# Chunk 0 of a linear-attention and PReLU kernel: scores and outputs as whole 128x128 products, k by tokens through transposes, longer idle products

## The chip, the cores and the metric

The kernel runs on one core of one Trainium2 chip. The metric is the device time of one execution in microseconds (us). The core has a TensorE (PE; its weight loads are listed as PEld), a VectorE (DVE), a ScalarE (ACT), a GpSimd (POOL) and a queue on SyncE (SP) that issues the DMAs. Each engine runs its own list of instructions in order and waits for the others by semaphores. TensorE's clock is granted at one of two levels, 2.4 GHz (1.00 in the profile) or 1.2 GHz (0.50).

## What is computed

```python
for t in range(S):                       # S = 768 tokens, B = 4, H = 8, D = 48
    kt, vt, rt = k[:, :, t], v[:, :, t], r[:, :, t]
    cur = einsum('bhd,bhe->bhde', u * kt, vt)
    y[:, :, t] = einsum('bhd,bhde->bhe', rt, state + cur)
    state = w * state + einsum('bhd,bhe->bhde', kt, vt)
x = y as (B*S, 384)
h = x @ w_in                             # 384 -> 2048
g = maximum(h, 0) + alpha * minimum(h, 0)
out = g @ w_out                          # 2048 -> 384
```

## The kernel before

The 768 tokens are cut into six chunks of 128. In each chunk the recurrence is written as products: r and k are scaled by powers of w (tables `W[m]`), the scores k.r of the chunk are masked to the strictly earlier tokens, their diagonal is filled with a sum over r.k.u, and the outputs are scores by v. What a chunk leaves behind is a state `T`, made of k by tokens (`kk`) and v. The eight heads go as four pairs, q = 0 to 3; a pair's two heads lie on partitions 0 to 47 and 64 to 111.

Chunk 0 has no state before it. `first_chunk` writes a pair's work: r and k0 are scaled on DVE (L431), their product is summed on PE (`c_sum`, L526) and goes through ACT to `cu` (L530). `scores` on PE works in half chunks of 64 tokens: 16 products of 64x64 for the two diagonal blocks (L445) and 8 for the block between them (L449). The mask's other side, `base`, is the identity times cu: four ACT instructions for one head (L462) and one DVE instruction for the other (L456, `BY_DVE`). DVE copies the masked scores over it (L466), ACT copies the block between to `off` (L470, shown as gl). `out` on PE (L480) takes 16 products for the tokens of the first half and then, behind an ACT reading of the same bank (`seen_y`, L486), 8 for the second half. The result is split in two terms (`xh`, `xl`) by ACT and by a PE product with minus the identity (`splits_by_pe`, L393), and DMAs (`lower`) bring one pair's rows to their places. `state` then writes k by tokens with real products against a diagonal matrix `spread` that holds w^128 (`by_tokens`, L298) and the state's own product (L508).

The two dense layers follow. They come as steps: `m_in` is nine products of 512 columns (L689), `m_out` nine more (L722); 96 steps, 1728 products. Their weights are unpacked on ACT and DVE (`weights`, L346 to L357), sixteen blocks, the first two while chunk 0 runs. The attention of chunks 1 to 5 is put between the steps in bursts (`burst`).

What sets the order: every piece of work is put into a plan with its engine, its cost in us and a rank (`add`); `in_order` walks through the pieces with those costs and writes one list for each engine. `warm` is an idle product: 256 columns of the identity into a spare bank, whose result nobody reads. `with_warm(n, ...)` puts n of them ahead of a piece, 33 stand at the start, and after planning each gap that the plan shows ahead of the first dense product gets more. Chunk 0's pairs 0 and 2 keep `base` in a pool of three buffers, which the masked scores of later chunks use too.

Of the kernel before, what the change touches and what calls it, by code (L numbers as in the profile page):

```python
# [18 lines left out]
L = 128  # L19
# [12 lines left out]
BY_DVE = (1,)  # L32
# [146 lines left out]
def rwkv_prelu_kernel(ctx: ExitStack, tc, rk, vkr, wP, uP, u, wall, alpha, w, r_all, k_all, v_all, oT):  # L179
# [26 lines left out]
    one, unit, ones = fixed([128, 2], "one"), sb([112, 65], "g", 3), sb([128, 128], "g", 3)  # L206
# [15 lines left out]
    const.tile([128, 32], F32, name="space")  # L222
# [8 lines left out]
    def warm(into):  # L231
        x = ident().bitcast(mybir.dt.bfloat16)
        nc.tensor.matmul(into()[:, 256:512], x[:, 0:128], x, start=True, stop=True, skip_group_check=True)  # L233

    def with_warm(n, us, fn, r, w, rank):

        p = add("PE", us + 0.107 * n, lambda: [warm(bank) for _ in range(n)] + [fn()], r=r + [ident] * (n > 0),
            w=w + [(bank, ("warm", len(plan.pieces)))] * (n > 0), rank=rank)
        p.warm = n

# [3 lines left out]
    def load(out, fn, kb, rank, behind=()):  # L244
# [19 lines left out]
        w=[ones], rank=-100)  # L264
    for g in range(2):
# [18 lines left out]
    def spreads():  # L284

        add("ACT", 0.3, lambda: nc.scalar.activation(minus(), ident()[0:112, 0:112], AF.Copy, scale=-1.0), r=[ident],
            w=[minus], rank=-60)
        for m in range(P):
            add("ACT", 0.3, lambda m=m: nc.scalar.activation(
                spread()[:, m], ident()[0:112].rearrange("p (g e) -> p g e", g=2)[:, :, 0:D], AF.Copy,  # L290
                scale=W[m]()[:, L:L + 1]), r=[ident, W[m]], w=[(spread, m)], rank=-59 + m)

    def by_tokens(q, k0, k, rank, behind=()):
# [7 lines left out]
        add("PE", 0.77, product, r=[k0, (spread, q)], w=[t], rank=rank).after.update(behind)  # L301
# [4 lines left out]
    def half_table():  # L306
# [3 lines left out]
        for m in range(P):  # L310
            for j in range(2):
                add("ACT", 0.3, lambda m=m, j=j: nc.scalar.activation(
                    rows()[:, m, HI * j:HI * (j + 1)], W[m]()[:, L - 1:HI - 1:-1], AF.Copy, scale=W[m]()[:, L:L + 1]), r=[W[m]],
                    w=[(rows, (m, j))], rank=-21).after.update(last_out)
        for m in range(P):
            add("PE", 0.15, lambda m=m: nc.tensor.transpose(
                pt()[:, 128 * m:128 * m + 112], rows()[:, m], ident()[0:112, 0:112]),
                r=[(rows, (m, j)) for j in range(2)] + [ident], w=[(pt, m)], rank=-20)
# [101 lines left out]
    def first_chunk(q):  # L420
# [17 lines left out]
        lo, hi = slice(0, HI), slice(HI, L)  # L438

        def scores():  # L440
            for b in range(B):
                at = slice(b * HI, (b + 1) * HI)
                for g in range(2):
                    for s in (lo, hi):
                        nc.tensor.matmul(A[g]()[s, at], k0()[half(g), b, s], r()[half(g), b, s], start=(b == 0),  # L445
                                         stop=(b == B - 1), skip_group_check=True)
            for b in range(B):
                for g in range(2):
                    nc.tensor.matmul(A[g]()[lo, 256 + b * HI:256 + (b + 1) * HI], k0()[half(g), b, lo], r()[half(g), b, hi],  # L449
                                     start=False, stop=(b == B - 1), skip_group_check=True)  # L450

        with_warm(3, 0.95, scores, r=[r, k0], w=A, rank=q - 90)
        base, off = sb([128, 2, B, HI], "base", 3), sb([128, 2, B, HI], "gl", 3, F32, mv)
        for g in range(2):
            if g in BY_DVE:
                add("DVE", 0.42, lambda g=g: nc.vector.tensor_tensor(  # L456
                    out=base()[:, g], in0=ident2()[:, None, :].broadcast_to([128, B, HI]),
                    in1=cu()[:, g, :, None].broadcast_to([128, B, HI]), op=ALU.mult), r=[cu, ident2],
                    w=[(base, (g, b)) for b in range(B)], rank=10 * q - 77 + g)
                continue  # L460
            for b in range(B):
                add("ACT", 0.32, lambda g=g, b=b: nc.scalar.activation(  # L462
                    base()[:, g, b], ident2(), AF.Copy, scale=cu()[:, g, b:b + 1]), r=[cu, ident2],
                    w=[(base, (g, b))], rank=-60 + q)
        for g in range(2):
            add("DVE", 0.44, lambda g=g: nc.vector.copy_predicated(  # L466
                base()[:, g], strict2()[:, None, :].broadcast_to([128, B, HI]),
                A[g]()[:, 0:256].rearrange("p (b t) -> p b t", b=B)), r=[strict2, A[g]],
                w=[(base, (g, b)) for b in range(B)], rank=10 * q - 76 + g)
            add("ACT", 0.42, lambda g=g: nc.scalar.activation(  # L470
                off()[lo, g].rearrange("p b t -> p (b t)"), A[g]()[lo, 256:512], AF.Copy), r=[A[g]], w=[(off, g)],
                rank=-59.5 + q)
        y = psum()

        def out(rows, pieces):
            for b in range(B):
                for g in range(2):
                    to, x = (lo if g == 0 else half(g)), g * B + b
                    for n, (t, j) in enumerate(pieces):
                        nc.tensor.matmul(y()[to, b * L + HI * j:b * L + HI * (j + 1)], v().rearrange("p x e -> p (x e)")[  # L480
                            rows, x * D:x * D + to.stop - to.start], t()[rows, g, b], start=(rows == lo and b == n == 0),
                            stop=(b == B - 1), skip_group_check=True)

        with_warm(2, 0.78, lambda: out(lo, ((base, 0), (off, 1))), r=[v, base, off], w=[y], rank=q - 85)

        add("ACT", 0.2, lambda: nc.scalar.activation(  # L486
            seen_y()[:, 0:2], y()[HI:HI + 1, B * L - 2:B * L], AF.Copy), r=[y], rank=-99)
        last_out[:] = [add("PE", 0.42, lambda: out(hi, ((base, 1),)), r=[v, base], w=[y], rank=q - 85.1)]
# [10 lines left out]
        def state():  # L499
            by_tokens(q, k0, k, -40 + q, last_out)  # L500
            U = psum()

            def product():
# [7 lines left out]
            add("PE", 0.47, product, r=[k, v], w=[U], rank=0.5 * q + 0.2)  # L511
            T[q] = sb([112, B, D], "T", 9)
            add("ACT", 0.4, lambda t=T[q]: nc.scalar.activation(t(), u_rows(U, 0), AF.Copy, scale=W[q]()[:, L:L + 1]),
                r=[U, W[q]], w=[T[q]], rank=0.5 * q + 0.2)
        return state

    def diagonal(q, r, k0, cu, sums, cols, mine, prod_rank, sum_rank, copy_rank):
# [11 lines left out]
        with_warm(3 if mine != sums else 0, 0.45, c_sum, r=[prod, uw], w=[mine], rank=sum_rank)  # L529
# [50 lines left out]
    def burst(i, was, at):  # L580
# [66 lines left out]
        first = add("PE", (0.7 if before else 0.1) + (0.8 if now else 0.1), run, r=uses, w=writes, rank=at)  # L647
        if before:

            row, col = (HI, L) if joint else (0, L)  # L650
            seen = add("ACT", 0.2, lambda: nc.scalar.activation(
                seen_y()[:, 0:2], y[1]()[row:row + 1, col + HI - 1:col + HI + 1], AF.Copy), r=[y[1]], rank=at - 200)
            seen.soon[first] = 0.75
# [29 lines left out]
    def m_in(n):  # L683
        c, i = STEPS[n]
        hp = psum("hp", 2)
        for k in range(NK):
# [6 lines left out]
            add("PE", 0.7, mm, r=[wh[i], wl[i]] + [(t[c], (kx, p)) for t in (xh, xl) for kx in need for p in range(6)],  # L693
# [266 lines left out]
```

## Time and profile before

| | us |
|---|---|
| median of three runs | 505.71 (504.98 to 506.17) |
| the profiled execution's own time | 506.03 |
| its span, first to last instruction | 504.3 |
| PE busy in the span | 492.1 (98%) |
| DVE, ACT, POOL busy | 310.8, 243.1, 41.9 |
| first dense product (L689) on PE | 44.6 after the span's start |

The page gives busy times over the whole span; views by stretch give each engine's busy time, the granted clock and the share of the DMA engines. In the chain of work that ended last each row is a start, a length and what ran then, and a row "issue" is time in which an engine waited for nothing that the profile shows. A product of 32-bit floats has two records in the trace, and one of the rounded kind that the dense layers use has one.

### The profile page before, as it was taken

Reading aid. Unit: us, or ns where it says so; the run is one execution under the profiler, and the core shown is the slowest. Engines: PE = TensorE matmul, PEld = TensorE weight load, DVE = VectorE, ACT = ScalarE, POOL = GpSimd, SP = SyncE. Lnnn points to the kernel's source line nnn. Section 1 sums busy time; section 2 is a strip of 40 time slices with the busy share of each in tenths; the row PEclk is TensorE's granted clock in tenths of the full one; section 3 lists DMA queues with packets and bytes.
Section 4 is the critical chain, followed back from the end, with each engine's and each line's share of the span. In section 5 each row is a group of like instructions: output and inputs, shape, how many; then the busy total and the mean of one; then the engine's idle time right before and its main releaser. Section 6 shows DMA issues by size and latency. Waiting matters only on the chain.

```text
span 504.3 us, 11838 instructions
## 1 busy us (share of the span) xinstructions
PE 492.1 (98%) x4949; PEld 404.8 (80%) x4949; DVE 310.8 (62%) x522; ACT 243.1 (48%) x565; POOL 41.9 (8%) x48
## 2 busy tenths in 40 slices
PE   8899999899999999999999999999999999999994
PEld 6688888678888888888888888888888887888883
DVE  7553988999988668586476466667544534333331
ACT  4556578566765555355345355444443324422222
POOL 1000001000321101110122020121000000000000
PEclk9856999999999999999999999999999999999999
DMA  7436267646314363141221131312030000100001
GB/s 216 160 89 207 99 199 217 183 164 215 108 50 154 101 199 113 56 147 39 89 74 53 53 130 48 97 57 69 20 96 1 1 1 1 63 0 1 0 1 68
DMA packets 23739, 45.87 MB, mean 91 GB/s; under 512 B 3968, under 2 KB 11264, under 8 KB 23680
## 3 DMA queue, kind: packets, MB, share of 16 engines
q1 hardware_dynamic: 23680, 45.05, 28.6%
q8 instruction: 41, 0.67, 0.6%
q14 instruction: 18, 0.15, 0.1%
HBM read 36.38 MB, written 6.29 MB: 85 GB/s over the span
## 4 chain that ended last, share of the span: by engine, by line
PE 95%; DVE 2%; DMA 1%; issue 1%; SPq 0%; ACT 0%; ACTq 0%
PE bank L689 39%; PE acc L722 39%; PE bank L627 3%; PE bank L637 2%; PE bank L298 2%; PE bank L480 2%; PE bank L606 2%; PE bank L599 2%; PE acc L233 1%; DMA raw<-rk 1%; PE bank L508 1%; PE bank L393 1%; DVE raw L549 0%; PE acc L526 0%; PE bank L526 0%
## 5 line engine op out<-in xcount | busy, mean ns | idle before, releaser
L698 DVE SCALAR_TENSOR_TENSOR g<-bank,alph,g 128x512 f32<-128x512 f32 x96 | 71.9, 749 | 109.8 <-ACT g L697 109.5
L697 ACT ACTIVATE g<-bank 128x512 f32<-128x512 f32 x96 | 57.2, 596 | 141.7 <-PE bank L689 141.5
L689 PE MATMUL bank<-xh,wh 128*128 128x512 f32 x288 | 113.5, 394 | 0.0
L689 PE MATMUL bank<-xh,wl 128*128 128x512 f32 x288 | 112.3, 390 | 0.0
L689 PE MATMUL bank<-xl,wh 128*128 128x512 f32 x288 | 112.1, 389 | 0.0
L702 DVE TENSOR_TENSOR gl<-g,gh 128x512 fp32r<-128x512 f32 x96 | 70.6, 736 | 38.3 <-ACT gh L701 37.6
L701 ACT ACTIVATE gh<-g 128x512 fp32r<-128x512 f32 x96 | 60.5, 630 | 64.2 <-DVE g L698 64.1
L722 PE MATMUL acc<-gh,wh 128*128 128x512 f32 x288 | 83.6, 397 | 1.6 <-ACT gh L701 1.6
L722 PE MATMUL acc<-gl,wh 128*128 128x512 f32 x288 | 81.4, 390 | 0.2 <-DVE gl L702 0.2
L722 PE MATMUL acc<-gh,wl 128*128 128x512 f32 x288 | 81.6, 390 | 0.0
L722 PEld LDWEIGHTS acc<-gl,wh 128*128 128x128 f32 x288 | 53.9, 188 | 11.9 <-DVE gl L702 0.7
L722 PEld LDWEIGHTS acc<-gh,wh 128*128 128x128 f32 x288 | 52.5, 188 | 13.5 <-ACT gh L701 2.4
L689 PEld LDWEIGHTS bank<-xl,wh 128*128 128x128 f32 x288 | 54.2, 188 | 11.3
L689 PEld LDWEIGHTS bank<-xh,wh 128*128 128x128 f32 x288 | 54.2, 188 | 11.4
L722 PEld LDWEIGHTS acc<-gh,wl 128*128 128x128 f32 x288 | 54.0, 188 | 11.5
L689 PEld LDWEIGHTS bank<-xh,wl 128*128 128x128 f32 x288 | 54.2, 188 | 11.1
L560 POOL TENSOR_TENSOR rr<-rr,kk 128x384 f32<-128x384 f32 x16 | 19.8, 1236 | 306.6 <-DMA kk<-vkr 164.7
L571 ACT ACTIVATE base<-ident,cu 128x64 f32<-128x64 f32 x160 | 41.3, 337 | 1.9 <-DVE cu L566 1.8
L382 DVE TENSOR_TENSOR xl<-bank,xh 48x256 fp32r<-48x256 f32 (+1 forms) x66 | 28.4, 430 | 3.8 <-ACT xh L381 2.5
L381 ACT ACTIVATE xh<-bank 48x256 fp32r<-48x256 f32 (+1 forms) x66 | 25.4, 385 | 2.9 <-PE bank L637 1.0
L549 DVE TENSOR_TENSOR raw<-raw,W 112x512 f32<-112x512 f32 x40 | 26.3, 680 | 0.8 <-DMA raw<-rk 0.8
L562 POOL TENSOR_TENSOR rr<-rr,utab 128x384 f32<-128x384 f32 x16 | 19.8, 1239 | 1.3
(107 smaller groups left out, 421.9 us busy)
## 6 DMA issues: line engine op xcount, KB each, us to landing
wraw<-wall SPq DMA_DIRECT2D x16, 768.0 KB, 4.6
raw<-rk SPq DMA_DIRECT2D x46, 224.0 KB, 3.6
v<-vkr SPq DMA_DIRECT2D x24, 192.0 KB, 3.8
kk<-vkr SPq DMA_DIRECT2D x16, 192.0 KB, 3.3
rr<-vkr SPq DMA_DIRECT2D x16, 192.0 KB, 2.5
oT<-o SPq DMA_DIRECT2D x12, 256.0 KB, 2.2
oT<-g SPq DMA_DIRECT2D x6, 256.0 KB, 2.6
xh<-xh SPq DMA_DIRECT2D x36, 32.0 KB, 2.0
```

What stands on the lines that cost most here:

```text
L381: add("ACT", us, lambda: nc.scalar.activation(to(h), view(), AF.Copy), r=[src], w=refs(h), rank=rank)
L382: add("DVE", us + 0.1, lambda: nc.vector.tensor_tensor(out=to(l), in0=view(), in1=to(h), op=ALU.subtract), r=[src] + refs(h), w=refs(l), r ...
L549: add("DVE", 0.72, lambda t=t, tab=tab: nc.vector.tensor_tensor(out=t().rearrange("p b (j t) -> p (b j) t", j=2), in0=t().rearrange("p b ( ...
L560: add("POOL", 1.2, lambda: nc.gpsimd.tensor_tensor(out=rt(), in0=rt(), in1=k(), op=ALU.mult), r=[k] + ([wh[12]] if c == 2 else []), w=[rt] ...
L562: add("POOL", 1.2, lambda: nc.gpsimd.tensor_tensor(out=rt().rearrange("p (g b) e -> p g b e", g=2), in0=rt().rearrange("p (g b) e -> p g b ...
L571: add("ACT", 0.32, lambda g=g, b=b: nc.scalar.activation(base()[:, g, b], ident2(), AF.Copy, scale=cu()[:, g, b:b + 1]), r=[cu, ident2], w ...
L689: nc.tensor.matmul(hp()[:, :], a[i]()[:, k], x[c]()[:, k], start=(k == 0 and j == 0), stop=(k == NK - 1 and j == 2))
L697: add("ACT", 0.6, lambda: nc.scalar.activation(g(), hp()[:, :], AF.Copy), r=[hp], w=[g], rank=n - 100)
L698: add("DVE", 0.75, lambda: nc.vector.scalar_tensor_tensor(out=g(), in0=hp()[:, :], scalar=alph()[:, i:i + 1], in1=g(), op0=ALU.mult, op1=A ...
L701: add("ACT", 0.64, lambda: nc.scalar.activation(gh(), g(), AF.Copy), r=[g], w=[gh], rank=n - 100)
L702: add("DVE", 0.73, lambda: nc.vector.tensor_tensor(out=gl(), in0=g(), in1=gh(), op=ALU.subtract), r=[g, gh], w=[gl], rank=n - 99)
L722: nc.tensor.matmul(banks[k](), a[i]()[:, NK + k], x(), start=(begin and j == 0), stop=(end and j == 2))
```

## The change

1. `scores` makes eight products of 128x128 a pair (L448 of the changed kernel) in place of 24 of 64x64, and `out` eight of K=128 and 128 columns (L469) in place of 24. The `seen_y` reading, `off` and its two ACT copies go.
2. `base` is a whole 128x128 block for each batch: eight ACT instructions a pair (L455), none on DVE; a pair takes two tiles of it, from the pool `base` for pairs 0 and 2, from `gl` for pairs 1 and 3. The two masked copies (L459) are 512 wide in place of 256.
3. Chunk 0's k by tokens is made by four plain transposes a pair and two ACT copies; w^128 comes in when the state leaves its bank (`w128`). Chunk 1 keeps `by_tokens`.
4. An idle product has 384 columns; a pair of chunk 0 has 2 + 2 + 3 + 2 = 9 of them in place of 8 of 256. The start has 23 in place of 33. A gap in the plan gets one for each 0.17 us, where it is over 0.25 us.
5. Costs in the plan change (dense products, bursts, the wait between a burst's halves), and so the order.

```diff
     def warm(into):
         x = ident().bitcast(mybir.dt.bfloat16)
-        nc.tensor.matmul(into()[:, 256:512], x[:, 0:128], x, start=True, stop=True, skip_group_check=True)
+        nc.tensor.matmul(into()[:, 128:512].rearrange("p (a f) -> p a f", a=2), x[:, 0:128],
+                         x[:, None, 0:192].broadcast_to([128, 2, 192]), start=True, stop=True, skip_group_check=True)
...
-        with_warm(3, 0.95, scores, r=[r, k0], w=A, rank=q - 90)
...
+        with_warm(2, 1.05, scores, r=[r, k0], w=A, rank=q - 90)
+        base = [sb([128, B, L], "gl", 3, F32, mv) if q % 2 else sb([128, B, L], "base", 3) for _ in range(2)]
+        for g in range(2):
+            for b in range(B):
+                add("ACT", 0.39, lambda g=g, b=b: nc.scalar.activation(
+                    base[g]()[:, b], ident(), AF.Copy, scale=cu()[:, g, b:b + 1]), r=[cu, ident], w=[(base[g], b)],
+                    rank=-60 + q)
...
+                    nc.tensor.matmul(y()[rows, b * L:(b + 1) * L], v().rearrange("p x e -> p (x e)")[
+                        :, x * D:x * D + rows.stop - rows.start], base[g]()[:, b], start=b == 0,
+                        stop=b == B - 1, skip_group_check=True)
+
+        last_out[:] = [with_warm(3, 0.95, out, r=[v] + base, w=[y], rank=q - 85)]
...
-            by_tokens(q, k0, k, -40 + q, last_out)
+            t = psum()
+
+            def turn():
+                for b in range(B):
+                    nc.tensor.transpose(t()[:, 112 * b:112 * (b + 1)], k0()[:, b], ident()[0:112, 0:112])
+
+            with_warm(2, 0.5, turn, r=[k0, ident], w=[t], rank=-40 + q).after.update(last_out)
...
-        with_warm(3 if mine != sums else 0, 0.45, c_sum, r=[prod, uw], w=[mine], rank=sum_rank)
+        with_warm(2 if mine != sums else 0, 0.56, c_sum, r=[prod, uw], w=[mine], rank=sum_rank)
...
-    add("PE", 7.0, lambda: [warm(bank) for _ in range(33)], r=[ident], w=[(bank, "warm")], rank=-1000)
+    add("PE", 6.7, lambda: [warm(bank) for _ in range(23)], r=[ident], w=[(bank, "warm")], rank=-1000)
```

The order on PE, ahead of the first dense product. Before, four pairs of real products (L298; rr is `spread`) and the states' products of the pairs stand there:

```order
L298 MATMUL bank_121<-rr,raw 128x96 x4
L298 MATMUL bank_119<-rr,raw 128x96 x4
L298 MATMUL bank_117<-rr,raw 128x96 x4
L298 MATMUL bank_118<-rr,o 128x96 x4
L508 MATMUL bank_121<-v,kk 64x48
L508 MATMUL bank_121<-v,kk 48x48
```

Now (L234 are idle products, L489 the transposes, L685 the dense ones, L503 the states' products):

```order
L489 MATMUL bank_117<-ident,raw 128x112 x4
L234 LDWEIGHTS ident
L234 MATMUL acc_135<-ident 128x384
...
L489 MATMUL bank_118<-ident,o 128x112 x4
L685 MATMUL bank_121<-xh,wh_82 128x512
L685 MATMUL bank_121<-xh,wl_98 128x512
L685 MATMUL bank_121<-xl,wh_82 128x512
L322 MATMUL bank_119<-ident,g 128x112 x2
```

The states' products, of which three pairs' stood ahead of the first dense product, all stand behind dense products now.

The order on ACT, from the first pair's cu on. Before, base for one head and the copies of the block between:

```order
L530 ACTIVATE cu<-acc_135 128x8
L462 ACTIVATE base<-ident_72,cu 128x64 x4
L470 ACTIVATE gl<-bank_117 64x256
L470 ACTIVATE gl<-bank_118 64x256
L530 ACTIVATE cu<-acc_135 128x8
```

Now:

```order
L525 ACTIVATE cu<-acc_135 128x8
L455 ACTIVATE base<-ident,cu 128x128 x7
L525 ACTIVATE cu<-acc_135 128x8
L455 ACTIVATE base<-ident,cu 128x128
L455 ACTIVATE gl<-ident,cu 128x128 x7
```

The second pair's cu moved ahead of the first pair's last piece of base; a pair has eight pieces in place of four and two copies.

## Rows read from the trace of the kernel before

**Rows 1.** The page: each engine's busy time, and PE's granted clock in 40 slices.
```profile
PE 492.1 (98%) x4949; PEld 404.8 (80%) x4949; DVE 310.8 (62%) x522; ACT 243.1 (48%) x565; POOL 41.9 (8%) x48
PEclk9856999999999999999999999999999999999999
```
**Rows 2.** Busy time by stretch: length, then engines (instructions), PE clock, DMA share, GB/s.
```profile
20.00:30.00 10.00, 9.18 (x133) 6.83 (x131) 3.93 (x9) 4.65 (x13) 0.00 (x0) 0.58 0.26 76
30.00:40.00 10.00, 10.00 (x79) 8.78 (x76) 4.81 (x6) 5.04 (x10) 0.00 (x0) 0.50 0.31 79
```
**Rows 3.** PE alone by stretch: length, busy (records), clock, DMA share, GB/s.
```profile
21.40:21.60 0.20, 0.20 (x14) 1.00 0.00 0
21.60:21.80 0.20, 0.20 (x7) 0.51 0.00 0
45.40:45.60 0.20, 0.20 (x2) 0.76 0.41 85
```
**Rows 4.** The chain that ended last, in order of time: start, length, what.
```profile
8.07 0.63 PE acc L526 x16
8.71 0.43 PE acc L233 x3
9.14 0.63 PE bank L445 x32
9.77 0.46 PE bank L449 x16
...
20.33 0.82 issue
...
22.39 1.93 PE bank L480 x31
...
34.27 7.07 PE bank L298 x32
...
44.61 1.32 PE bank L689 x3
45.94 0.29 PE bank L316 x3
...
109.00 2.04 PE acc L722 x9
```
**Rows 5.** PE's instructions in order of time: start, length, what.
```profile
33.16 1.11 PE L480 MATMUL bank<-base,v 64*64 64x64 f32 x16
48.54 0.67 PE L508 MATMUL bank<-v,kk 128*64 128x48 f32 x16
```
**Rows 6.** ACT's instructions in order of time.
```profile
9.18 0.18 ACT L530 ACTIVATE cu<-acc 128x8 f32<-128x8 f32 x1 [4.73 <-PE acc L233]
10.43 0.62 ACT L470 ACTIVATE gl<-bank 64x256 f32<-64x256 f32 x2
19.70 0.89 ACT L346 ACTIVATE wx<-wraw 128x768 f32<-128x768 f32 x1
22.50 0.59 ACT L392 ACTIVATE xh<-bank 112x512 fp32r<-112x512 f32 x1
74.28 2.02 ACT L571 ACTIVATE base<-ident,cu 128x64 f32<-128x64 f32 x8
```
**Rows 7.** DVE's instructions in order of time.
```profile
5.26 0.55 DVE L282 RECIPROCAL W<-W 112x64 f32<-112x64 f32 x1
7.85 1.28 DVE L431 TENSOR_TENSOR raw<-raw,W 112x512 f32<-112x512 f32 x2
10.90 0.77 DVE L466 COPY_PREDICATED base<-strict,bank 128x256 f32<-128x256 uint8 x2
22.98 0.95 DVE L350 SCALAR_TENSOR_TENSOR wx<-wraw,wx 128x768 uint32<-128x768 uint32 x1
46.26 0.56 DVE L319 COPY whalf<-bank 128x384 f32<-128x384 f32 x1 [8.33 <-PE bank L316]
```
**Rows 8.** Busy time by stretch, columns as in Rows 2: the fullest of DVE.
```profile
106.00:116.00 10.00, 10.00 (x46) 8.29 (x45) 9.97 (x15) 7.62 (x14) 0.00 (x0) 1.00 0.57 215
```

More of the change, by code (lines that the diff above doesn't have):

```diff
@@ L264, in rwkv_prelu_kernel @@
         w=[ones], rank=-100)
+    add("POOL", 0.3, lambda: nc.gpsimd.tensor_copy(strict(), ones()), r=[ones], w=[strict], rank=-60)
     for g in range(2):
@@ L299, in product @@
                                  start=True, stop=True, skip_group_check=True)
-        add("PE", 0.77, product, r=[k0, (spread, q)], w=[t], rank=rank).after.update(behind)
+        add("PE", 0.92, product, r=[k0, (spread, q)], w=[t], rank=rank)
         add("ACT", 0.5, lambda: nc.scalar.activation(
@@ new lines, in first_chunk @@
+        with_warm(2, 1.05, scores, r=[r, k0], w=A, rank=q - 90)
[5 more added lines that the diff above has]
+                    rank=-60 + q)
+        for g in range(2):
+            add("DVE", 0.73, lambda g=g: nc.vector.copy_predicated(
+                base[g](), strict()[:, None, :].broadcast_to([128, B, L]),
+                A[g]()[:, :].rearrange("p (b t) -> p b t", b=B)), r=[strict, A[g]], w=[base[g]],
+                rank=10 * q - 76 + g)
@@ L447, in scores, with out @@
+        y = psum()
+        def out():
             for b in range(B):
                 for g in range(2):
-                    nc.tensor.matmul(A[g]()[lo, 256 + b * HI:256 + (b + 1) * HI], k0()[half(g), b, lo], r()[half(g), b, hi],
-                                     start=False, stop=(b == B - 1), skip_group_check=True)
-        with_warm(3, 0.95, scores, r=[r, k0], w=A, rank=q - 90)
[L453 to L488, printed above, removed]
+                    rows, x = (slice(0, HI) if g == 0 else half(g)), g * B + b
+                    nc.tensor.matmul(y()[rows, b * L:(b + 1) * L], v().rearrange("p x e -> p (x e)")[
+                        :, x * D:x * D + rows.stop - rows.start], base[g]()[:, b], start=b == 0,
+                        stop=b == B - 1, skip_group_check=True)
@@ L645, in run @@
                 products()
-        first = add("PE", (0.7 if before else 0.1) + (0.8 if now else 0.1), run, r=uses, w=writes, rank=at)
+        us = {(1, 1): 3.0 if before and joint else 2.05, (1, 0): 1.8 if before and joint else 1.25, (0, 1): 1.5}
+        first = add("PE", us[before is not None, now is not None], run, r=uses, w=writes, rank=at)
         if before:
-            row, col = (HI, L) if joint else (0, L)
+            row, col = (HI, 3 * L) if joint else (0, L)
             seen = add("ACT", 0.2, lambda: nc.scalar.activation(
                 seen_y()[:, 0:2], y[1]()[row:row + 1, col + HI - 1:col + HI + 1], AF.Copy), r=[y[1]], rank=at - 200)
-            seen.soon[first] = 0.75
+            seen.soon[first] = 1.7 if joint else 1.05
             add("PE", 0.3, lambda: through_scores(1), r=[v0, base0], w=y[joint:], rank=at - 200)
@@ L692, in m_in @@
             need = range(NK) if c and k == 0 else (k,)
[L693 removed]
+            add("PE", MM, mm, r=[wh[i], wl[i]] + [(t[c], (kx, p)) for t in (xh, xl) for kx in need for p in range(6)],
                 w=[hp], rank=n)
@@ L725, in m_out @@
             for k in range(NK):
-                add("PE", 0.7, lambda k=k: [mm(j, (k,)) for j in range(3)], r=[wh[i], wl[i], gh, gl], w=[banks[k]],
+                add("PE", MM, lambda k=k: [mm(j, (k,)) for j in range(3)], r=[wh[i], wl[i], gh, gl], w=[banks[k]],
                     rank=n + MLAG - 0.5)
@@ L818, in rwkv_prelu_kernel @@
         if p.eng == "PE":
-            begun = begun or p.rank >= 0 and p.us == 0.7
+            begun = begun or p.us == MM
             gap = 0.0 if last is None else max(0.0, p.start - last - 0.05)
-            if not begun or p.takes and gap > 0.3:
-                fill[p] = int(gap / 0.125), p.takes[0] if begun else bank
+            if gap > 0.25 and (not begun or p.takes):
+                fill[p] = int(gap / 0.17), p.takes[0] if begun else bank
             last = p.end
```

49 lines of the change are left out of this document (27 added, 22 removed).

## The prediction

> **What bounds the kernel now.** I read the page first: PE is busy for 98% of the span, so the end is set by what PE has to do and at which clock, and only the second to fourth of the 40 clock slices are short of full [rows 1]. The views by stretch place it: PE is busy without a pause from 30 to 40 us at a clock of 0.50, while DVE has 4.8 us of work in those ten and ACT 5.0 [rows 2]. Finer stretches put the fall at 21.6 us and the return at 45.5 [rows 3], 23.9 us at half speed. What PE did before the fall is in the chain: small products, and a pause of 0.82 us at 20.33 for which the profile shows no waiting [rows 4]. What it did before the rise: the first 512-column products, from 44.61 on. In between, a busy PE alone did not bring the clock back: 7.07 us of L298 without a gap ran at 0.50 to the end [rows 4]. DVE, meanwhile, stood idle for 8.33 us behind PE's transposes [rows 7]. So the stage to change is the one from 8.07 us (the first c_sum) to 44.61 (the first dense product); everything behind it is a chain of dense products at 2.04 us for nine [rows 4], whose end moves with its start as long as DVE, which is full in places (9.97 of 10 us) [rows 8], keeps up.
>
> **The change part by part.** I work out when the first dense product now starts if the clock holds, on PE, and then look whether ACT or DVE is later.
>
> PE, at full speed, a pair at a time. *c_sum* is unchanged, 0.56 to 0.63 us; I take 0.60 [rows 4]. *Scores*: the old block between, eight products of 64 columns in two row halves, took 0.46 [rows 4]; eight of 128 columns in the same two halves should take twice that, 0.92; if the halves no longer ran side by side it would be 1.84. I take 0.95, beside 0.63 + 0.46 = 1.09 before. *Out*: before, 1.93 + 1.11 us at half clock [rows 4, 5], so 1.52 at full; 24 x 64 = 1536 columns become 8 x 128 = 1024 in the same two column halves, so 1.52 x 2/3 = 1.0; upper bound 1.52, no gain at all, lower bound 0.92 as for the scores. *Transposes*: three took 0.29 among dense products [rows 4], so four are 0.39; upper bound is the old real products, 7.07 / 4 / 2 = 0.88. I take 0.45, near the row of the same instruction. *Idle products*: in the list there are 35 from the first c_sum to the first dense product. Three of 256 columns take 0.43, 0.143 each [rows 4]; one and a half times that is 0.215, while 384 columns at the rate of the dense products (2.04 / 9 = 0.227 for 512) are 0.17. I take 0.20, so 7.0 us (6.0 to 7.5). Three products with minus the identity at 0.23 and one small one are 0.9.
> Sum: 4 x (0.60 + 0.95 + 1.0 + 0.45) = 12.0, + 7.0 + 0.9 = 19.9; 8.07 + 19.9 = 28.0. The bounds give 26.1 (0.56, 0.92, 0.92, 0.39, idle 6.0) and 36.0 (0.63, 1.84, 1.52, 0.88, idle 7.5).
> The opening is neutral: 25 idle products of 384 columns in place of 36 of 256 are 9600 columns for 9216.
>
> ACT. base is 32 pieces of 128x128 in place of 16 of 128x64 and eight copies of 64x256. A 64-wide piece takes 2.02 / 8 = 0.25, a 256-wide copy 0.62 / 2 = 0.31 [rows 6]; nothing shows a 128-wide one, I take 0.29 (0.25 to 0.39, the upper end with a tenth added for a cost that grows with the length faster than these two say). From the first cu at 9.18: 4 x 0.18 + 32 x 0.29 = 10.0, one xh (0.59) and one wx (0.89) that stand between them, 0.5 for the new copies of w^128: 21.2 (19.9 to 24.4). A wait is added: base of pairs 2 and 3 takes buffers that pairs 0 and 1 must give back, the fifth to eighth pieces of each wait for an `out` of PE, and xh and wx of the weights are queued on ACT around them. By the PE sum those outs are done near 16 and 20 us, when ACT comes there, so I cost it at nothing; if PE is late, it is late by the same.
>
> DVE. From 7.85: five scalings and three products for c_sum at 0.64, a reciprocal 0.55, eight masked copies of 512 (two of 256 took 0.77, so at most 0.77 each; plain 512-wide work takes 0.64; I take 0.70), chunk 1's first scaling 0.64 and two steps of the weights at up to 0.95 [rows 7]: 5.1 + 0.55 + 5.6 + 0.64 + 1.9 = 13.8, done at 21.7. The cover is thin: PE itself is at the last `out` at 28.0 - 4 x (0.45 + 0.40) - 1.0 - 0.2 = 23.4, so ACT (21.2 and a copy of 0.7) and DVE are 1.5 us ahead of it. I add 1.0 for waits that this overlap will not hide: first dense product at 29.0, in place of 44.6.
>
> Behind it: the first dense block needs wl of weights block 0, which before was done long ahead; DVE has four steps of the weights at up to 0.95 to do ahead of and with it behind the last masked copy, near 4 us, so it comes near 27. That is late but not last. From 44.61 back to 29.0 is 15.6. Of this the states' products of three pairs, moved behind dense products, are paid later at full clock: 3 x 0.65 [rows 5] = 1.9. The dense products between 44.6 and 45.5 ran at half clock, which gives 0.4. Net 14.1. The bursts of chunk 1 are in another order; PE is busy for 98% of the span [rows 1], so the new order can lose more than it gains, and DVE has little left [rows 8]. I charge 1.1 and bound it by 2 gained and 4 lost. So 13.0 off the profiled execution: 506.03 - 13.0 = 493.0. That execution lies 0.3 above the median of the runs, 505.71, so the forecast is **492.7 us**.
>
> Against the transposes speaks a rule. No row shows what transposes alone do to the clock: the old ones stood among dense products at full clock [rows 4]. The Trainium skill (TensorE: Matmul & The Clock Gate, Part 4: PE-mode transpose) says that transposes do not count as busy for the clock as other products do. By it the last stretch before the dense products would rest on its eight idle products alone; the forecast takes those to be enough, and rival 1 is what it costs if not.
>
> **The rivals.**
> 1. The clock falls late, in the transposes (from about 24 us on). For it: there is hardly anything but transposes and idle products there, and the busy L298 did not bring the clock back. Against it: eight idle products of 384 columns in these 4 us, where by the list eight of 256 and the pause stood between the third pair's scores and the fall. Price: 4.6 us of PE work at half speed, and the first dense products with it, +5.5: 498.
> 2. The change does not hold the clock at all: it falls near 21 us as now, because of a pause like that at 20.33, whose cause no row shows. Then what is left, 7 us of PE's sum, takes 14, +7: 499.7. For it: the pause was not a wait on another engine, so nothing in the change takes it away. Against: with 8 instead of 24 products for each scores and out there are fewer instructions, and more idle columns around it.
> 3. DVE or ACT takes PE's place: a base piece costs 0.39 (3 us more), or the dense stage waits for weights because DVE starts it with less in hand. Then some 4 us of the gain go: 496.7. For it: the thin cover above and DVE's 9.97 [rows 8].
> 4. Slower: the clock falls in the opening, at pair 1 (about 11 us), since there the list has six idle products of 256 a pair before and four of 384 now, which are no more columns, and the work between them is less. Then 17 of the 19.9 us double: the first dense product comes at 46, and the states' products still have to be paid: 46 - 44.6 + 1.9 = 3.3, less the 0.4, plus 1.1: 509.7. It ends slower than before if the fall comes before about 15 us, 13 us of PE work ahead of the dense products. Against it: in that stretch the old kernel held the clock with the same columns.
>
> **How the numbers follow.** Forecast 0.62 (490 to 495.5), rival 1 0.14, rival 2 0.08, rival 3 0.10, rival 4 0.06. The range reaches from 489 (the lower PE bound, 1.9, and the new order gaining 2) to 499.5, which takes in rivals 1 and 3 and the upper PE bound if the cover is then free (36.0 - 29.0 = 7.0 on 492.7), and leaves out rival 4 and half of rival 2. A measurement of this kernel can tell about 0.2% from no change, 1.0 us. Faster by more: all but rival 4, and a little for several mishaps at once, 0.92; the same 0.02; slower 0.06.
>
> **What would show it.** Right: the granted clock at 1.00 in all stretches from 8 us on; the first L685 at 27 to 31; L448 at about 0.95 a pair, L469 at 1.0, L489 at 0.4 to 0.5; the ACT pieces at 0.29; the last masked copy at 22 to 24; L503 at 0.65 each behind the first dense products. Rivals 1 and 2 show as 0.50 between 21 and 35, rival 3 as waits of PE on base or wl, rival 4 as 0.50 near 11. The forecast is wrong in its size if the dense stage no longer runs without stalls: then the first dense product is early and the end is not.

## The result, and the profile after

The changed kernel takes 490.88 us (median of four executions, 490.47 to 491.73), the kernel before, in four executions beside it, 505.52 (504.98 to 506.17). The ratio is 0.971, with a 95% interval of 0.969 to 0.973. The profiled execution takes 490.48 us, 15.55 less than that of before, where the prediction took 13.0 off; the forecast was 492.7. Of 20 further executions of the kernel before beside the experiments, 18 had a mean granted clock of 0.959 to 0.978 and took 504.0 to 512.3 us, and two had 0.996 and 0.998 and took 497.1 and 494.9, against which the change brings 4 to 6 us and not 14.6. Below, times are compared with times.

The page of the changed kernel, lines as in [rows 1]:

```profile
PE 478.6 (98%) x4665; PEld 390.2 (80%) x4665; DVE 308.6 (63%) x518; ACT 246.1 (50%) x573; POOL 45.9 (9%) x49
PEclk9999999999999999999999999999999999999999
```

PE is as full as before, but busy for 13.5 us less, and none of the 40 slices is short of its clock. The stretches that stood at 0.58 and 0.50 in [rows 2] are now, with the columns named there:

```profile
20.00:30.00 10.00, 9.80 (x91) 6.71 (x88) 8.18 (x14) 9.85 (x26) 0.00 (x0) 1.00 0.17 39
30.00:40.00 10.00, 9.60 (x114) 7.75 (x115) 7.67 (x12) 7.91 (x21) 0.00 (x0) 1.00 0.89 280
```

The clock is full in both. ACT, which had 4.65 of 10 us between 20 and 30, has 9.85, and DVE 8.18 in place of 3.93: in a stretch where only PE was full, ACT is now as full as PE, and DVE not far from it. The steps of chunk 0 on PE in order of time (start, length, what); the distance from one start to the next is what a step costs, since lengths overlap:

```profile
8.45 0.63 PE L521 MATMUL acc<-uw,g 112*64 112x2 f32 x16 [0.71 <-DVE g L514]
9.01 0.50 PE L234 MATMUL acc<-ident 128*128 128x384 bf16 x2
9.44 1.16 PE L448 MATMUL bank<-raw 48*128 48x128 f32 x16
10.53 0.50 PE L234 MATMUL acc<-ident 128*128 128x384 bf16 x2
...
16.16 1.09 PE L469 MATMUL bank<-base,v 128*64 128x128 f32 x16
17.18 0.50 PE L234 MATMUL acc<-ident 128*128 128x384 bf16 x2
...
24.55 1.09 PE L469 MATMUL bank<-gl,v 128*64 128x128 f32 x16
...
26.23 0.55 PE L489 MATMUL bank<-ident,raw 112*128 112x112 f32 x4
26.61 0.49 PE L234 MATMUL acc<-ident 128*128 128x384 bf16 x2
...
28.73 0.50 PE L685 MATMUL bank<-xh,wh 128*128 128x512 f32 x1
```

The first dense product starts at 28.73. In the same view of the kernel before it starts at 44.54 (44.61 in the chain of [rows 4], which begins a step where the one before it ends). The last dense product starts 453 us later in both (before, then after):

```profile
44.54 0.80 PE L689 MATMUL bank<-xh,wh 128*128 128x512 f32 x1
...
497.49 0.39 PE L722 MATMUL acc<-gl,wh 128*128 128x512 f32 x1
```

```profile
481.73 0.39 PE L718 MATMUL acc<-gl,wh 128*128 128x512 f32 x1
```

That is 15.76 us earlier, so the dense stage, from its first product's start to its last one's, is as long as it was: 453.00 us, and before 452.95. All of the gain lies ahead of it. The same two starts, the landmarks from here on, can be read in each experiment. They leave out what follows the last product's start within the span, which is 5.5 to 7.1 us in the profiles of this case; but they are those of one execution.

| kernel | median us (range) | first dense product | last one | between |
|---|---|---|---|---|
| before | 505.5 (505.0 to 506.2) | 44.5 | 497.5 | 453.0 |
| changed | 490.9 (490.5 to 491.7) | 28.7 | 481.7 | 453.0 |
| e1_idle_only | 496.6 (496.2 to 497.2) | 35.8 | 488.7 | 452.9 |
| e9_idle_turn | 497.0 (495.8 to 500.4) | 33.7 | 488.2 | 454.5 |
| e2_idle_256 | 490.6 (489.4 to 490.7) | 28.0 | 481.8 | 453.8 |
| e3_turn_bare | 490.7 (490.6 to 493.2) | 29.0 | 484.3 | 455.2 |
| e4_no_idle | 491.3 (490.5 to 492.3) | 27.5 | 482.7 | 455.1 |
| e7_cold | 496.7 (496.5 to 498.6) | 29.8 | 488.3 | 458.5 |
| e5_real_tokens | 490.8 (490.3 to 493.5) | 30.5 | 483.3 | 452.8 |
| e6_old_costs | 491.2 (490.1 to 492.1) | 28.6 | 483.0 | 454.4 |
| e8_pool_base | 493.3 (492.1 to 494.3) | 30.6 | 484.5 | 453.9 |
| e10_pool_idle | 492.3 (490.0 to 493.6) | 29.4 | 483.6 | 454.3 |

The starts are those of the profiled execution of each. That was the longest of the four for e3 (493.2 us) and e6 (492.1), and the shortest for e9 (495.8). No "between" is under 452.8. What is above it can be waits or half clock in the dense stage, but its work is not quite the same in all of them either, since the states' products stand in it in some and ahead of it in others.

### The profile page after: what moved, and what is told of

Its sections match the earlier page's. It is cut to its first block, busy times and chain, and to the rows that moved or that the text cites. A ratio compares the mean times of both kernels' runs of the same rounds, so it can differ in the third digit from the quotient of the medians.

```text
span 488.5 us, 11281 instructions
## 1 busy us (share of the span) xinstructions
PE 478.6 (98%) x4665; PEld 390.2 (80%) x4665; DVE 308.6 (63%) x518; ACT 246.1 (50%) x573; POOL 45.9 (9%) x49
## 3 DMA queue, kind: packets, MB, share of 16 engines
q1 hardware_dynamic: 23680, 45.05, 29.8%
## 4 chain that ended last, share of the span: by engine, by line
PE 88%; DVE 5%; DMA 3%; ACT 1%; SPq 1%; issue 0%; ACTq 0%
PE acc L718 40%; PE bank L685 38%; PE bank L622 2%; PE bank L632 2%; DMA raw<-rk 2%; PE bank L601 2%; PE bank L594 1%; DMA wraw<-wall 1%; PE acc L234 1%; DVE raw L544 1%; DVE wx L356 1%; DVE wx L359 1%; PE bank L469 1%; DVE g L514 1%; DVE wl L363 1%; DVE gl L698 0%
## 5 line engine op out<-in xcount | busy, mean ns | idle before, releaser
L685 PE MATMUL bank<-xh,wh 128*128 128x512 f32 x288 | 113.0, 392 | 0.0
L685 PE MATMUL bank<-xh,wl 128*128 128x512 f32 x288 | 112.1, 389 | 0.0
L685 PE MATMUL bank<-xl,wh 128*128 128x512 f32 x288 | 112.1, 389 | 0.0
L718 PE MATMUL acc<-gh,wh 128*128 128x512 f32 x288 | 83.4, 397 | 0.0
L718 PE MATMUL acc<-gh,wl 128*128 128x512 f32 x288 | 81.8, 391 | 0.0
L718 PE MATMUL acc<-gl,wh 128*128 128x512 f32 x288 | 81.4, 390 | 0.0
L685 PEld LDWEIGHTS bank<-xh,wh 128*128 128x128 f32 x288 | 54.1, 188 | 11.4
L718 PEld LDWEIGHTS acc<-gl,wh 128*128 128x128 f32 x288 | 54.0, 188 | 11.3
L685 PEld LDWEIGHTS bank<-xl,wh 128*128 128x128 f32 x288 | 54.0, 188 | 11.2
L718 PEld LDWEIGHTS acc<-gh,wl 128*128 128x128 f32 x288 | 53.8, 188 | 11.4
L685 PEld LDWEIGHTS bank<-xh,wl 128*128 128x128 f32 x288 | 54.1, 188 | 11.0
L718 PEld LDWEIGHTS acc<-gh,wh 128*128 128x128 f32 x288 | 52.7, 188 | 11.3
L555 POOL TENSOR_TENSOR rr<-rr,kk 128x384 f32<-128x384 f32 x16 | 24.6, 1540 | 287.4 <-DMA kk<-vkr 162.5
L653 DVE COPY_PREDICATED base<-strict,bank 128x256 f32<-128x256 uint8 x40 | 17.2, 443 | 4.4 <-PE bank L601 4.4
```

Source lines behind the costliest of these rows:

```text
L555: add("POOL", 1.2, lambda: nc.gpsimd.tensor_tensor(out=rt(), in0=rt(), in1=k(), op=ALU.mult), r=[k] + ([wh[12]] if c == 2 else []), w=[rt] ...
L653: add("DVE", 0.42, lambda g=g: nc.vector.copy_predicated(base()[:, g], strict2()[:, None, :].broadcast_to([128, B, HI]), A[g]()[:, 0:256]. ...
L685: nc.tensor.matmul(hp()[:, :], a[i]()[:, k], x[c]()[:, k], start=(k == 0 and j == 0), stop=(k == NK - 1 and j == 2))
L718: nc.tensor.matmul(banks[k](), a[i]()[:, NK + k], x(), start=(begin and j == 0), stop=(end and j == 2))
```

## The experiments

**The idle products alone: e1_idle_only.** The kernel before, with 384 columns in an idle product and as many of them in the pairs and at the start as the change has; plan and order stay.

```diff
-        nc.tensor.matmul(into()[:, 256:512], x[:, 0:128], x, start=True, stop=True, skip_group_check=True)
+        nc.tensor.matmul(into()[:, 128:512].rearrange("p (a f) -> p a f", a=2), x[:, 0:128],
+                         x[:, None, 0:192].broadcast_to([128, 2, 192]), start=True, stop=True, skip_group_check=True)
...
-    add("PE", 7.0, lambda: [warm(bank) for _ in range(33)], r=[ident], w=[(bank, "warm")], rank=-1000)
+    add("PE", 7.0, lambda: [warm(bank) for _ in range(23)], r=[ident], w=[(bank, "warm")], rank=-1000)
```

> The kernel before with the idle products alone changed: 384 columns, nine a pair, placed as in the changed kernel; every real product, the plan and the order stay. Theory (the gain is mostly the clock, and the idle products hold it): 1.00 from 8 us on, and PE's work up to the first dense product at full speed is 4 x (0.60 + 1.09 + 1.52 + 0.88) + 36 idle ones at 0.20 + 0.9 + 1.9 for three pairs of states' products = 26.4, so it starts near 34.5 in place of 44.6; with 0.4 for the dense products that were slow, 495. Rival (the clock needs the whole products, or falls with the pause of 0.82 us whatever the idle products are): it falls near 21 us as before and the time is 504 to 508.

Measured: 496.58 us (ratio 0.982, 0.978 to 0.986). By stretch:

```profile
20.00:30.00 10.00, 9.60 (x182) 6.91 (x178) 6.40 (x12) 6.72 (x18) 0.00 (x0) 1.00 0.34 101
30.00:40.00 10.00, 10.00 (x120) 8.72 (x118) 5.29 (x8) 8.43 (x21) 0.00 (x0) 1.00 0.62 175
```

The clock holds, the small products of 64 columns notwithstanding, and 9 us are gone. That agrees with the two executions of the kernel before in which the mean clock was full (497.1 and 494.9). So the half clock between 21.6 and 45.5 us [rows 3] cost about 9 us, and the other 5.7 us of the change are something else.

What they are can be read from PE's starts in the two profiles, 7.0 us between the two first dense products. An out takes 1.72 us a pair in e1 (1.11 and 0.61) and 1.02 in the changed kernel: 4 x 0.70 = 2.8. K by tokens takes 0.87, a pair's transposes 0.38: 4 x 0.49 = 2.0. The states' products of three pairs, 1.66, moved behind dense products. A pause of 0.40 and an L317 of 0.25 are gone too. That is 7.1; the scores give nothing (1.09 in both). The states' products are only moved, and paid later. The theory had 495 for e1, and its first dense product 1.3 us earlier (34.5 for 35.8).

**The old idle products in the changed kernel, and none: e2_idle_256 and e4_no_idle.** e2 is the changed kernel with 256 columns in an idle product again and 33 at the start; e4 has no idle product in chunk 0 behind the start's 23. The order is the changed kernel's in both.

```diff
-        p = add("PE", us + WARM * n, lambda: [warm(bank) for _ in range(n)] + [fn()], r=r + [ident] * (n > 0),
+        p = add("PE", us + WARM * n, lambda: [fn()], r=r + [ident] * (n > 0),
```

> The changed kernel with idle products of 256 columns again, at the same places and in the same number (33 at the start, so that the opening is as long); plan and order stay. If the length of the idle products is what holds the clock: a fall between 20 and 29 us and 495 to 500. Rival (whole products and the missing pause are enough): 1.00 throughout, and 35 x 0.054 = 1.9 us less on PE, of which ACT and DVE let through at most 0.5 us: 490.4 to 490.9.

> The changed kernel without any idle product behind the opening's 23; plan and order stay. Theory (idle products are what holds the clock): a fall before 16 us; of PE's 19.9 us 7 are gone, and 10 of the rest run at half speed, so the first dense product comes at 31 to 34: 494 to 497. Rival (the whole products hold the clock by themselves): 1.00 throughout and 490.3 to 491, since ACT and DVE set the start of the dense stage.

Measured: 490.6 us for e2 (0.970, 0.966 to 0.974), and 491.3 for e4 (0.972, 0.968 to 0.976). The clock of e4 by stretch (length, PE busy and records, clock, DMA share, GB/s):

```profile
12.00:16.00 4.00, 2.74 (x48) 1.00 1.03 344
...
24.00:28.00 4.00, 2.96 (x27) 1.00 0.22 48
```

PE is busy for only three quarters of these stretches, without one idle product, and the clock stays at 1.00 in the execution that was profiled. In the three others of e4 the mean clock was 0.991, 0.983 and 0.983 (0.998 in the profiled one), and they took 492.31, 490.62 and 491.98 us, hardly more. In e2 it was 0.996 to 0.999 in all four. So the theory that the longer idle products are what holds the clock in the changed kernel falls: in the kernel before they do it (e1), here those of the old length are enough (e2). Without any (e4) the clock held in one execution, and in three it was short somewhere, where it cost little; where, no trace shows.

e4 also shows what PE would gain by not doing 6.9 us of idle products: its first dense product is 1.2 us earlier, and its last one 0.9 later. What PE waited for (us in total, times, longest):

```profile
PE acc L521 <- DVE g L514: 2.1, 2, 1.2
...
PE bank L632 <- ACT seen_y L647: 1.3, 1, 1.3
PE bank L469 <- DVE base L459: 1.3, 1, 1.3
PE bank L305 <- DVE raw L544: 1.2, 1, 1.2
PE bank L685 <- ACT kk L493: 1.0, 1, 1.0
```

The idle products stand in time that PE would else wait. Ahead of the first dense product it waits for ACT and DVE. Behind it the wait for DVE's raw (L305) is not for DVE's own work: DVE stood idle itself, for a transfer of chunk 1's r and k (rk). The changed kernel's DVE, the piece of its chain that ended last, and the same two for e4:

```profile
35.03 0.69 DVE L544 TENSOR_TENSOR raw<-raw,W 112x512 f32<-112x512 f32 x1 [1.44 <-DMA raw<-rk]
30.21 4.79 DMA raw<-rk
...
35.13 0.69 DVE L544 TENSOR_TENSOR raw<-raw,W 112x512 f32<-112x512 f32 x1 [2.24 <-DMA raw<-rk]
29.83 5.28 DMA raw<-rk
```

With the first dense product 1.2 us earlier the transfer starts only 0.4 earlier, and it ends no earlier. In the changed kernel, too, PE's L305 starts at 35.83, 0.1 behind the end of that DVE step.

**The transposes without idle products: e3_turn_bare.** The eight idle products ahead of the transposes go, as the rule that the prediction's first rival stands on would have it matter.

```diff
-            with_warm(2, 0.5, turn, r=[k0, ident], w=[t], rank=-40 + q).after.update(last_out)
+            with_warm(2, 0.5, turn, r=[k0, ident], w=[t], rank=-40 + q, real=0).after.update(last_out)
```

> The changed kernel without the eight idle products ahead of the transposes; plan and order stay. If transposes do not hold the clock and nothing else does there: a fall between 24 and 29 us, transposes at twice 0.39, the first dense products at half speed: 491.5 to 494. Rival (the stretch is too short for a fall): 1.00 throughout; the 8 x 0.2 us are not won, since ACT and DVE deliver the dense product's inputs no earlier than 28.2: 490.3 to 490.9.

Measured: 490.7 us (0.972, 0.967 to 0.976). The stretch and its products:

```profile
24.00:32.00 8.00, 6.77 (x50) 1.00 0.30 58
```

```profile
26.21 1.31 PE L489 MATMUL bank<-ident,raw 112*128 112x112 f32 x12
27.39 0.60 PE L489 MATMUL bank<-ident,o 112*128 112x112 f32 x4
29.03 0.50 PE L685 MATMUL bank<-xh,wh 128*128 128x512 f32 x1 [1.03 <-ACT kk L493]
```

Sixteen transposes in a row (in two rows, of 12 and 4) and a wait of 1.03 us behind them leave the clock at 1.00. ACT's copies (kk) come 1.0 us after PE is done, so the first dense product is even a little later.

**No idle products at all: e7_cold.** As e4, and one in place of 23 at the start.

```diff
-    add("PE", 6.7, lambda: [warm(bank) for _ in range(23)], r=[ident], w=[(bank, "warm")], rank=-1000)
+    add("PE", 6.7, lambda: [warm(bank) for _ in range(1)], r=[ident], w=[(bank, "warm")], rank=-1000)
```

> The changed kernel without any idle product, the opening's too (one is left): PE comes to chunk 0 cold. What the clock is worth to the changed kernel. If PE runs at half speed up to the dense stage: 12.9 us of work take 25.8 and the first dense product comes at 34 to 36, 496 to 499. Rival (ACT and DVE set the pace so far that even a half-speed PE keeps up): first dense product by 30, 491 to 492.5. If the whole products raise the clock by themselves: 1.00 from some point between 8 and 20 us, 490.5 to 493.

Measured: 496.7 us. PE's instructions in order of time, and the clock by stretch:

```profile
15.29 2.08 PE L448 MATMUL bank<-raw 48*128 48x128 f32 x16
...
19.54 1.16 PE L448 MATMUL acc<-o 48*128 48x128 f32 x16
```

```profile
20.00:24.00 4.00, 3.15 (x49) 1.00 0.04 10
24.00:28.00 4.00, 3.29 (x22) 0.73 0.18 41
...
64.00:68.00 4.00, 4.00 (x18) 0.65 0.20 41
```

The scores take 2.08 us in the third pair and 1.16 in the fourth: PE began at half speed and came to full speed without an idle product, on whole products and the c_sums between them. In the kernel before, 23.9 us of smaller products, PE busy throughout from 30 to 40 us, did not bring it back [rows 2, 3]. It fell again near 25.9, behind a wait of 1.56 us. The time is in the range of the first theory, but not for its reason: the first dense product comes at 29.8, not at 34 to 36. Against e4 the opening's idle products are worth 5.4 us, and the ones in the pairs nothing that these times can tell. Only 2.3 of this lie ahead of the first dense product. The dense stage is 3.4 longer, and in it PE stands still from 58.98 to 61.78 for nothing that the profile shows, and then has half clock near 63 to 67. What the opening has to do with that pause is not shown.

**The transposes without the rest, and the rest without them: e9_idle_turn and e5_real_tokens.** e9 is e1 with k by tokens through transposes and w^128 in the state's evacuation; e5 is the changed kernel with the real products back in chunk 0.

```diff
-            by_tokens(q, k0, k, -40 + q, last_out)
...
+            with_warm(2, 0.556, turn, r=[k0, ident], w=[t], rank=-40 + q).after.update(last_out)
```

> The kernel before with the idle products as in the run of idle products alone and, besides, the transposes for k by tokens with w^128 in the state's evacuation; scores and outputs stay in half chunks. With PE as the bound (it was busy without a pause to the first dense product in that run) the transposes take 4 x (0.87 - 0.38) = 2.0 us off 496.6: 494.4 to 494.9. Rival (ACT or DVE takes over): 495.5 to 496.6. The rest down to the changed kernel's 490.9 is then the whole products and the states' products behind the first dense ones.

> The changed kernel with the real products for k by tokens in chunk 0 again, in the transposes' place with the same two idle products and the same cost in the plan. Theory now (with the whole products PE is no longer late: ACT and DVE bring the dense stage's inputs at about 28, and PE's 28.7 is only just behind): 4 x (0.87 - 0.38) = 2.0 us more PE work at the end of PE's chain show in full: 492.5 to 493. Rival (PE has slack there): 490.5 to 491.

Measured: e9 497.0 us, e5 490.8. In e9 the first dense product is 2.1 us earlier than in e1, as PE's sum has it, and the last one only 0.5; the median is above the ranges of both the theory and the rival. One of PE's waits in e9, the piece of its chain behind which it stands, and DVE's step; then, from e1, the issue of the same transfer:

```profile
PE bank L304 <- DVE raw L565: 1.5, 1, 1.5
33.32 3.81 DMA raw<-rk
37.15 0.69 DVE L565 TENSOR_TENSOR raw<-raw,W 112x512 f32<-112x512 f32 x1 [1.58 <-DMA raw<-rk]
...
33.57 0.58 SPq L408 DMA_DIRECT2D raw<-rk  x1
```

The wait for DVE's raw is not in e1's list. It is again the transfer of chunk 1's r and k: SP issues it only 0.25 us earlier than in e1, so DVE stands idle for it and PE for DVE. In the changed kernel the step shows in the landmarks: undone in e5, both come later, by 1.8 and 1.6 us. The median doesn't show it (490.8 against 490.9); in the profiled executions what follows the last product took 5.5 us in e5 and 6.8 in the changed kernel. With four executions each this is left unresolved in the time. What the time does show is the whole products: e1 and e5 both have the longer idle products and the old k by tokens, and e5, with whole products and the new plan, is 5.8 us quicker (what the plan's costs bring, the next run prices).

**The planner's costs: e6_old_costs.** The changed kernel with the old costs of a dense product, of a burst and of its second half's wait, and with the old column for the ACT reading `seen_y` behind a burst. Up to the first dense product the order is the same.

```diff
-MM = 0.682
+MM = 0.7
...
-            seen.soon[first] = 1.7 if joint else 1.05
+            seen.soon[first] = 0.75
```

> The changed kernel with the planner's costs as they were before: a dense product's cost of 0.7 in place of the lower one, and the old price of a score's wait. Up to the first dense product the order stays the same, behind it some rows change places. Theory (the order behind the first dense product is worth nothing, the 1.1 us that the prediction took off for it was not there in net): 490.5 to 491.5 us, the second part product's transfer from the first dense product at 105 to 106 us as in both kernels. Rival (the new costs take out stalls that the changed kernel would else have): 492 to 495, with new waits of TensorE for VectorE or ScalarE in the dense stretch.

Measured: 491.2 us (490.1 to 492.1). The last dense product is 1.3 us later than in the changed kernel, behind a wait of L305 for ACT of 0.9. The last transfer of an o into part is issued 105.7 us behind the first dense product in the kernel before (150.3) and in the changed one (134.4), and 107.5 behind it in e6 (136.1), later than the theory has it. The time is within the theory's interval, so the two don't agree: the new order is worth 0.3 us by the medians and 1.3 by the landmark of e6's longest execution. It is no loss.

**Less for ACT: e8_pool_base and e10_pool_idle.** The second head's base is made by one GpSimd instruction in place of four ACT ones; e8 without idle products (as e4), e10 with them. The order changes, since the planner sees the new cost.

```diff
+            if g == 1:
+                add("POOL", 1.3, lambda g=g: nc.gpsimd.tensor_tensor(
+                    out=base[g](), in0=ident()[:, None, :].broadcast_to([128, B, L]),
+                    in1=cu()[:, g, :, None].broadcast_to([128, B, L]), op=ALU.mult), r=[cu, ident],
+                    w=[(base[g], b) for b in range(B)], rank=-60 + q)
+                continue
```

> A try at a faster kernel: the changed kernel without the idle products of chunk 0 (the 23 at the start stay), and base of the second head made by one POOL instruction of 512 columns a pair in place of four on ACT; the plan orders anew. If ACT's queue is what sets the start of the dense stage: 16 x 0.29 = 4.6 us less on ACT, of which DVE lets through about 2: first dense product near 26, 488.5 to 489.5. If DVE and the weights' DMAs set the stage behind it anyway: 490 to 491. If POOL takes over 3 us for an instruction: later masked copies, 491 to 494.

> The changed kernel, idle products kept, and the base that ScalarE adds for the second head of a pair made by one GpSimd instruction of 128x512 in its place, so that ScalarE has about 1 us less of it up to 24 us. Theory (ScalarE binds from 20 to 30 us, but the weights' transfer and VectorE behind it take the gain back): 490.5 to 491.5 us, ScalarE under 9.5 of 10 us in 20 to 30, the last landmark on TensorE within 0.4 us of the changed kernel's. Rival 1 (ScalarE alone binds there): 489 to 490. Rival 2 (GpSimd's instruction is late, TensorE's first dense product waits for it): 491.5 to 494.

Measured: 493.3 us for e8, slower than the changed kernel, and 492.3 for e10, whose four executions (490.0 to 493.6) reach into the changed kernel's range. GpSimd's instruction takes 1.26 to 1.57 us in e8, not the 3 that its slow case had. ACT has 8.79 of 10 us in e10 from 20 to 30, and the first dense product is not earlier (29.4). The clock falls in both; e10 and then e8 by stretch, PE only:

```profile
32.00:36.00 4.00, 3.15 (x52) 0.95 1.03 296
36.00:40.00 4.00, 4.00 (x27) 0.62 0.97 251
```

```profile
12.00:16.00 4.00, 2.09 (x42) 1.00 1.08 354
16.00:20.00 4.00, 2.38 (x28) 0.53 0.55 182
```

Ahead of the fall PE had waited in e10 (busy 3.15 of 4 us), and in e8 the fall came in a wait of 2.48 us (busy 2.09 and 2.38). Whether ACT alone would bind with the order kept can't be told from these two, since order and clock moved with it. None of the ten kernels beats the changed one by more than the times can tell.

## Why the prediction was right, and where it was not

**What bounds, and PE's sum: right.** From the first c_sum to the first dense product PE needs 20.3 us (19.9 was forecast): c_sum 0.56 a pair (0.60), out 1.02 (1.0), transposes 0.38 (0.45), 35 idle products at 0.196 (0.20, 6.9 in all), products with minus the identity and the small one 1.2 (0.9). One term was mis-sized: the *scores*, forecast at 0.95 from the old 64-column block, take 1.09, just what the 24 smaller products took; there is no gain in them. The work begins at 8.45, 0.4 late behind DVE's g, and the 1.0 us charged for waits was not there. So the start at 28.73, forecast at 29.0, is in part luck: 0.4 too little for PE's work and 0.4 for its late begin stand against 1.0 too much.

**ACT and DVE: late, and still covered.** ACT's base pieces came as forecast, but both queues ended later than the 21.2 and 21.7 us worked out. The changed kernel's ACT and DVE in order of time:

```profile
9.76 2.15 ACT L455 ACTIVATE base<-ident,cu 128x128 f32<-128x128 f32 x7
...
21.58 1.27 ACT L455 ACTIVATE gl<-ident,cu 128x128 f32<-128x128 f32 x4
```

```profile
23.18 0.72 DVE L459 COPY_PREDICATED gl<-strict,acc 128x512 f32<-128x512 uint8 x1
```

Seven pieces take 2.15 us, 0.3 each (0.29 forecast); the last ones stand behind xh and wx and end at 22.9. The last masked copy ends at 23.9, and the last out begins at 24.55: 0.65 us of cover where the prediction had 1.5. PE waited for neither behind its first c_sum. e4 shows what happens when that cover is gone.

**Behind the first dense product: the step that failed.** The prediction took 15.6 us for the earlier start, and then took off 1.9 for the moved states' products, gave back 0.4, and charged 1.1 for the order: 2.6 us in all. The dense stage has in truth kept its length, 453.00 us for 452.95. Two views of the 105.4 us from the first dense product on, grouped by line (busy time and mean ns of one, then idle time ahead of them), before and then after; both stretches hold the same 185 products of L689 (L685) and 162 of L722 (L718):

```profile
L722 PE MATMUL acc<-gh,wh 128*128 128x512 f32 x54 | 15.8, 400 | 1.6 <-ACT gh L701 1.6
...
L508 PE MATMUL bank<-v,kk 128*64 128x48 f32 (+1 forms) x17 | 1.0, 225 | 0.0
L233 PE MATMUL bank<-ident 128*128 128x256 bf16 x5 | 0.7, 275 | 0.0
```

```profile
L632 PE MATMUL bank<-base,v 64*48 64x64 f32 x128 | 5.3, 218 | 0.5 <-ACT seen_y L647 0.5
...
L305 PE MATMUL bank<-rr,raw 112*128 112x96 f32 x32 | 4.3, 278 | 0.7 <-issue 0.7
...
L503 PE MATMUL bank<-v,kk 128*64 128x48 f32 (+1 forms) x64 | 2.5, 220 | 0.0
...
L322 PE MATMUL bank<-ident,g 112*128 112x112 f32 x4 | 1.0, 287 | 0.2 <-ACT g L318 0.2
```

The states' products are paid, as forecast: 2.5 us where there was 1.0. Against them PE no longer does 0.7 us of idle products there nor waits 1.8 us for gh and gl (0.2 of it for gl); it waits 1.4 elsewhere. With the 0.4 that the half clock cost there before, these come to 1.5 as well, though sums of busy times that overlap can't be closed to a tenth. The charge of 1.1 for the new order had no row behind it, and e6 has the new order as no worse than the old one. This is the 2.55 us by which the profiled execution was quicker than forecast: 2.6 not lost, 0.2 more at the start (15.8 for 15.6), and 0.2 back outside the span, which is 15.8 shorter where the time is 15.55.

**The clock: the fact right, the reason only in part.** The forecast rested on longer idle products holding the clock. e1 shows that they do so in the kernel before. In the changed kernel e2 shows that the old length is enough, and e4 that the time hardly needs idle products in the pairs at all: either part of the change is enough. So the parts don't add up: the idle products alone bring 9 us, and with whole products there next to nothing is left for them to bring.

**The rivals.** The first, a fall in the transposes, did not come, with idle products between them or without (e3). The Trainium skill (TensorE: Matmul & The Clock Gate, Part 4: PE-mode transpose), on whose rule it stood, says that transposes don't count as busy for the clock as other products do; here 1.7 us of nothing else ran at 1.00, and what a longer stretch does no run shows. The second and fourth are out by the clock of 1.00 from 8 us on. The third, ACT or DVE in PE's place, is not what happened, but it is next: e3 and e4 have waits on these two of 0.9 to 1.3 us ahead of the first dense product as soon as PE is some 1 to 2 us quicker. Neither the prediction nor a rival had the transfer of chunk 1's r and k, on which DVE and PE stand behind it in e4 and e9.

## What to carry to other kernels

A loss by a fallen clock and a loss by more work than needed are priced apart: first what the stretch would take at full clock, with the old products, then what fewer instructions save at that clock; here 9 and 5.7 us, where two parts of the change each keep the clock from costing time and only one can be paid for it. Add the work of a stage up for every engine at its new speed, and keep the cover in sight: 0.65 us was left, and savings on PE ahead of the dense stage (e2, e4) came back as waits. Where the named engine itself stood idle, follow the wait one step further: twice it was a transfer, which starts hardly earlier when PE does. A charge for "the order may be worse" needs a row; between two landmarks that both kernels have, the trace tells afterwards whether anything was lost in that execution, where the executions' times lie 1 us and more apart.

## What was not expected of the hardware

A busy PE is not enough to bring the clock back, and an idle product is not needed for it. In the kernel before, ten us without a pause at 0.50 [rows 2] changed nothing; in e7, whole products and c_sums took PE from half speed (2.08 us for a pair's scores) to full (1.16). And a pause is not enough for a fall: e4 waits 1.27 us near 19.5 at 1.00, and e1 has the pause for nothing visible that [rows 4] shows at 20.33, of 0.40 us at 20.8, without a fall; the kernel before, e7 and e10 fell behind theirs, and e8 in the middle of one. What separates them is open, as is the cause of the "issue" pauses, of which e7 has one of 2.8 us at 59.

The clock's column can be wrong at the start: the page of e7 has a full first slice of 12 us, in which a group of products takes nearly twice its later time (scores 2.08 for 1.16, c_sum 1.02 for 0.59).

```profile
PEclk9989989999999999999999999999999999999999
```

The length of a known instruction is the check.

Whole products of 128 columns take as long for the scores as three times as many of 64 (1.09 us a pair both ways), but the outs, with 128 rows to sum over in place of 64, go from 1.72 to 1.02. Why the two differ no run shows.
